# Spectral filter and squared-ReLU feed-forward, two layers on one core: paired evictions of the inverse transform, split banks for the first two tiles, outer and inner quarters for the last tile of layer 1

## The chip, the core and the metric

The kernel runs on one core of a Trainium2 chip. The core's engines work through their own lists of instructions and wait for each other by semaphores: TensorE (PE in the profile, its weight loads PEld), VectorE (DVE), ScalarE (ACT), GpSimd (POOL) and SyncE (SP, which here issues most of the DMAs). Matrix products go to PSUM, which has eight banks of 512 float32 per partition, and ACT or DVE copy them from there to SBUF ("evict" them). The metric is the device time of one execution in microseconds (us), as the median of several runs.

## The reference

`x` is 2048 x 448 in bf16. Four blocks follow one another; A is a spectral filter with a residual, B a feed-forward network with a residual, and each has its own normalisation in front:

```python
def _A_ref(x, w_r, w_i):
    X = rfft2(x.astype(float32), axes=(-2, -1))
    X = X * (w_r + 1j * w_i)
    return irfft2(X, s=(S, D), axes=(-2, -1)).astype(bfloat16)

def _B_ref(x, w1, b1, w2, b2):
    h = einsum("bsd,df->bsf", x, w1) + b1
    r = where(h > 0, h, 0)
    return einsum("bsf,fd->bsd", r * r, w2) + b2

x = x + _A_ref(_layernorm(x), A_w_r, A_w_i)
x = x + _B_ref(_layernorm(x), B_w1, B_b1, B_w2, B_b2)
x = x + _A_ref(_layernorm(x), A_w_r, A_w_i)
x = x + _B_ref(_layernorm(x), B_w1, B_b1, B_w2, B_b2)
```

S is 2048, D is 448, the filter's weights are 2048 x 225, and the hidden width is 1792.

## The kernel before

**Tiling.** The sequence index is split as 128 partitions times 16 tiles, `s = 16 p + t`, so a tile `t` holds every sixteenth row. A transform of length 2048 is then one of length 128 over partitions and one of length 16 over tiles. Along D the code first forms sums and differences of `x[d]` and `x[447-d]`, and for layer 2 of their halves again, so that the products over D have 224 or 112 columns (`HD` = 224, `QD` = 112).

**Stages of a spectral block.** `A1` (layer 1) and `A2` (layer 2) normalise a tile and make the first transform: a tile's statistics (`ln_stats`, `act_stats`, `ln_rstd`) give a scaled copy `Fs` of the constant matrix `FA_sb`, on POOL, ACT or DVE; the products go to a bank and are evicted to `XA`. `TD` is the transform over D of one pair of the eight pairs of sequence frequencies, evicted to the arena. `B` is the part over 16, evicted to the arena as well. `W` multiplies by the complex weights `Wt`, all on DVE. `Bi` is the inverse over 128: for a pair p two banks (`lb` 0 and 1) of four matmuls each, evicted to `VT`. `TI` is the inverse over D by tiles, evicted to `TIo` (in the profile `tmp`), and `AI` the last inverse step, added to `x` by DVE into `x_sb` (L1104). The pairs run in the order 1 to 7, 0; `Bi0.n` is the n-th in layer 1, `Bi1.n` in layer 2, so n = 7 is pair 0. A pair's Bi needs W's products for that pair.

**Stages of a feed-forward block.** `ln_B` squares and sums a tile (`Square` with an accumulator, L1128, on ACT) and sets up the normalisation; the tile is transposed into `yT` (by matmuls for tiles 0 and 1, later by DMA). `h` makes the hidden columns: matmuls with `W1_sb`, relu on ACT, square on DVE. The first hidden matmuls (`h0.0`, `h1.0`) need tiles 0 and 1 alone. `o` multiplies by `W2_sb` and adds the residual (L1245, `o_tile`). In layer 1 each `o` tile is followed by its `A2` work for layer 2: `ln_stats`, sums and differences into `xin`, a second level of them into `yA`, and `second_A`'s four matmuls of 128 columns into a bank, evicted to `XA` by ACT. The last tile, t = 15, has its 448 output columns cut into two halves (`CUT`), so that the first half's work overlaps the second half's matmuls. `TD1.0` is the first that needs `XA` of all 16 tiles.

**What sets the order.** The program is written as a list of small units of work, numbered as they are created, each with its engine, its reads and writes, and a cost. A planner can order them by those costs, but here `ORDER` holds a finished order: for each engine the unit numbers in the sequence in which they are issued, PE, ACT, DVE, POOL and SP each on its own. `EV` and `op.alt` say which engines may take a unit; the list in which its number stands decides. Costs and priorities (`PR`) therefore do not change what is issued. Banks are handed out along that order. `warm_mm` (L1352) adds matmuls on ones that only keep PE busy: 16 at the start, 9 more in waits.

**Start.** POOL clears `ones`, then the last block of `W1_sb`, makes the indices `ix`, gathers two blocks of the filter's weights by indirect DMA, makes four reversed copies of x (`XR`), clears the padding of `x_sb`, and then scales the first `Fs`. The clearing of the padding of `Z` in the arena (128 x 1024) is its last instruction. SP issues the loads one after another and holds the two loads of `Wt` that wait for the gathers, and what stands behind them. `b1in` (the bias of the hidden layer) is loaded early; its transposing matmul stands between layer 1's TD and B products, before TD0.5.

Of the kernel before, what the change touches and what calls it, by code (L numbers as in the profile page):

```python
# [6 lines left out]
ALU = mybir.AluOpType  # L7
# [17 lines left out]
VB_PAIRS = (2, 3, 4, 5)  # L25

# [98 lines left out]
1384 1389 1394 1399 1410 1404 1407 1413 1416""",  # L125
    "act": """
# [12 lines left out]
1306 1308 1303 1170 1171 1174 1177 1178 1377 1372 1370 1380 1375 1387 1382 1385 1392 1390 1397 1395 1400 1402""",  # L139
    "dve": """  # L140
# [108 lines left out]
def _res(a):  # L249
    return a.ap() if isinstance(a, _PsAP) else a  # L250
# [1180 lines left out]
```

## Time and profile before

| | us |
|---|---|
| median of 3 runs | 269.94 |
| lowest, highest | 269.80, 269.97 |
| profiled execution | 269.8 |
| its span in the profile | 267.9 |
| granted clock of PE | 1.00 |

The page of the profile gives busy times over the whole span. PE is busy for nearly all of it, so what matters more is the busy time by stage: a stage whose PE column nearly equals its length is bound by PE, and in the others another engine's column, or a chain between the engines, sets the length. The seams are: 0 to 18.6 us the loads, statistics and A1; to 43.5 TD, B, W and Bi of layer 1; to 56.4 TI and AI with the first hidden matmuls; to 137.1 the feed-forward network; to 146.3 the last tile and the rest of A2; to 161.5 TD, B and W of layer 2; to 168.9 Bi1; to 175.5 TI and AI up to the first hidden matmul; to 265.5 the second network; and then the last store.

In a timeline row the columns are the start, the time until the last of the grouped instructions ends, the engine, the line, the operation, the tiles, the shapes and the count. In square brackets stands how long the engine had been idle before, and which engine and line ended that.

### The profile page before, as it was taken

The numbers are of one execution on the slowest core, as the hardware profiler recorded it, in microseconds if no ns is written. First come the engines' busy times: TensorE is split into PE (matmuls) and PEld (weight loads), VectorE is DVE, ScalarE is ACT, GpSimd is POOL, SyncE is SP. The second block draws the span as 40 slices with busy tenths as digits, with TensorE's granted clock in tenths as the row PEclk, the third lists the DMA queues.
The fourth block names the chain that finished last, engine by engine and source line by source line (L and its number), as shares of the span: only waits on it lengthen the run. The fifth ranks groups of instructions, "written<-read, shape, count | busy, mean of one in ns | idle before, by whom it ended". The sixth has DMA issues, their size and how long they took to land.

```text
span 267.9 us, 5691 instructions
## 1 busy us (share of the span) xinstructions
PE 256.9 (96%) x2090; PEld 165.1 (62%) x2090; DVE 203.7 (76%) x724; ACT 175.6 (66%) x393; POOL 14.9 (6%) x31
## 2 busy tenths in 40 slices
PE   8789998999999999999998998899999999999996
PEld 3667587778544555655567766688654675554454
DVE  3978996999999976299997899689995059734442
ACT  5977899987279746784226897899445885040930
POOL 8940000000000000000000000000000000000000
PEclk9999999999999999999999999999999999999999
DMA  7999410022300215000000000001423100023103
GB/s 232 404 291 347 157 40 1 3 40 42 66 10 20 41 22 107 4 0 2 1 0 2 2 0 0 4 14 30 78 60 68 42 0 0 20 39 92 52 0 103
DMA packets 25554, 16.33 MB, mean 61 GB/s; under 512 B 18186, under 2 KB 24566, under 8 KB 25528
## 3 DMA queue, kind: packets, MB, share of 16 engines
q1 hardware_dynamic: 24792, 14.26, 19.7%
q10 hardware_dynamic: 576, 0.92, 0.9%
q0 software_dynamic: 160, 0.81, 0.7%
q8 instruction: 16, 0.26, 0.4%
q14 instruction: 10, 0.08, 0.1%
HBM read 10.46 MB, written 1.84 MB: 46 GB/s over the span
## 4 chain that ended last, share of the span: by engine, by line
PE 76%; DVE 11%; ACT 7%; POOL 2%; issue 2%; DVEq 0%; ACTq 0%; POOLq 0%
PE ps L675 76%; ACT VT L700 4%; DVE tmp L729 4%; DVE arena L729 2%; DVE x_sb L1104 1%; ACT arena L700 1%; POOL Wt L772 1%; DVE x_sb L1245 1%; ACT arena L694 1%; DVE VT L729 1%; ACT XA L700 1%; DVE st L834 1%; POOL VT L701 1%; POOL W_sb L742 1%; ACT VT L1128 0%
## 5 line engine op out<-in xcount | busy, mean ns | idle before, releaser
L675 PE MATMUL ps<-yT,W_sb 64*128 64x512 bf16 (+1 forms) x770 | 90.2, 346 | 0.1
L675 PE MATMUL ps<-W_sb,arena 128*128 128x448 bf16 (+3 forms) x476 | 87.1, 342 | 0.0
L675 PEld LDWEIGHTS ps<-yT,W_sb 64*128 64x128 bf16 (+1 forms) x770 | 56.2, 95 | 30.3 <-ACT arena L694 1.6
L675 PEld LDWEIGHTS ps<-W_sb,arena 128*128 128x128 bf16 x476 | 45.5, 98 | 38.5 <-DVE arena L729 1.6
L729 DVE TENSOR_TENSOR arena<-arena 128x512 bf16<-128x512 bf16 (+1 forms) x140 | 45.2, 365 | 25.3 <-ACT arena L694 24.9
L694 ACT ACTIVATE arena<-ps,b1col 128x512 bf16<-128x512 f32 x84 | 51.7, 692 | 18.1 <-PE ps L675 17.9
L1128 ACT ACTIVATE VT<-x_sb 128x448 bf16<-128x448 bf16 x32 | 18.5, 581 | 22.4 <-DVE x_sb L1104 22.4
L700 ACT ACTIVATE arena<-ps 128x448 bf16<-128x448 f32 (+1 forms) x42 | 26.2, 723 | 6.0 <-PE ps L675 5.9
L1245 DVE SCALAR_TENSOR_TENSOR x_sb<-ps,arena 128x448 bf16<-128x448 f32 (+3 forms) x26 | 14.7, 582 | 12.5 <-PE ps L675 12.2
L694 ACT ACTIVATE mv<-mv,epst 128x1 f32<-128x1 f32 (+1 forms) x41 | 11.7, 296 | 16.9 <-DVE mv L835 10.8
L700 ACT ACTIVATE XA<-ps 128x512 bf16<-128x512 f32 x28 | 15.3, 594 | 6.0 <-PE ps L675 5.9
L694 ACT ACTIVATE arena<-ps 128x256 bf16<-128x256 f32 x56 | 17.8, 400 | 1.3 <-PE ps L675 1.3
L675 PE MATMUL ps<-arena,G_sb 128*128 128x448 bf16 (+1 forms) x84 | 17.0, 335 | 0.4 <-ACT arena L700 0.4
L675 PE MATMUL ps<-H_sb,arena 128*128 128x256 bf16 x128 | 16.2, 273 | 1.2 <-DVE arena L729 0.8
L675 PE MATMUL ps<-yT,VT 64*128 64x512 bf16 x42 | 15.8, 376 | 0.0
L700 ACT ACTIVATE VT<-ps 128x512 bf16<-128x512 f32 (+1 forms) x30 | 14.5, 631 | 1.4 <-PE ps L675 1.4
L729 DVE TENSOR_TENSOR tmp<-arena,Wt 128x896 bf16<-128x896 bf16 x26 | 14.8, 622 | 0.4 <-ACT arena L700 0.4
L675 PEld LDWEIGHTS ps<-H_sb,arena 128*128 128x128 bf16 x128 | 11.9, 98 | 5.1 <-DVE arena L729 3.3
L700 ACT ACTIVATE tmp<-ps 128x896 bf16<-128x896 f32 (+1 forms) x18 | 14.1, 850 | 1.4 <-PE ps L675 1.4
L675 PE MATMUL ps<-TD_sb,XA 112*128 112x112 bf16 (+1 forms) x184 | 13.9, 229 | 1.0 <-ACT XA L700 1.0
L675 PEld LDWEIGHTS ps<-TD_sb,XA 112*128 112x128 bf16 (+1 forms) x184 | 12.3, 98 | 2.8 <-DVE XA L701 1.2
L1104 DVE SCALAR_TENSOR_TENSOR x_sb<-ps,x_sb 128x448 bf16<-128x448 f32 x16 | 9.8, 620 | 4.5 <-PE ps L675 4.5
(89 smaller groups left out, 295.4 us busy)
## 6 DMA issues: line engine op xcount, KB each, us to landing
out_dram<-x_sb SPq DMA_DIRECT2D x15, 112.0 KB, 1.8
W_sb<-in_B_w_dram SPq DMA_DIRECT2D x1, 1568.0 KB, 10.1
W_sb<-in_B_w_dram SPq DMA_DIRECT2D x1, 1344.0 KB, 10.3
xin<-in_A_x_dram ACTq DMA_DIRECT2D x4, 224.0 KB, 4.8
xin<-in_A_x_dram SPq DMA_DIRECT2D x4, 224.0 KB, 4.2
H_sb<-c_H SPq DMA_DIRECT2D x1, 896.0 KB, 9.4
G_sb<-c_G SPq DMA_DIRECT2D x1, 672.0 KB, 7.9
Wt<-in_A_w_i_dram SPq DMA_DIRECT2D x1, 393.8 KB, 7.3
```

The costliest lines, as they stand in the source:

```text
L675: return sch.add("pe", lambda e: e.matmul(_res(o), lhsT, rhs, start=start, stop=stop, skip_group_check=skip), [lhsT, rhs], [o], cost=cost, ...
L694: sch.add("act", lambda e: e.activation(o, _res(i), func, **kw), rd, [o], cost=c)
L700: op = sch.add(engs[0], lambda e: e.activation(o, _res(i), ACT.Copy) if h[0].eng == "act" else e.tensor_copy(o, _res(i)), [i], [o], cost=c ...
L701: e.tensor_copy(o, _res(i)), [i], [o], cost=c[engs[0]], unit=unit)
L729: sch.add(eng, lambda e: e.tensor_tensor(o, _res(a), b, op), [a, b], [o], cost=_free(o) / rate + 69.0)
L742: sch.add(eng, lambda e: e.memset(o, v), [], [o], cost=_free(o) / 1.92 + 60.0)
L772: sch.add("pool", lambda e: e.indirect_dma_start(o, None, (A_w_r, A_w_i)[i], bass.IndirectOffsetOnAxis(ix[:], 0)), [ix[:]], [o], is_dma=Tr ...
L834: small(lambda e, si=si, xi=xi: e.bn_stats(si, xi), [xi], [si], _free(xi) / 0.96 + 69.0)
L1104: small(lambda e, xx=xx, xi=xi, r=r, i=i: e.scalar_tensor_tensor(out=xx, in0=_res(r), scalar=1.0, in1=xi, op0=ALU.mult, op1=ALU.add, accum ...
L1128: sch.add("act", lambda e, i=i, o=o, x=x: e.activation(o, x, ACT.Square, accum_out=sd[:, i, 1:2]), [x], [o, sd[:, i, 1:2]], cost=560.0)
L1245: small(lambda e: e.scalar_tensor_tensor(out=o, in0=_res(i), scalar=r[0] if r else 1.0, in1=xb[:, t, d0:d1], op0=ALU.mult, op1=ALU.add), [ ...
```

## The change

1. `MERGE`: for the Bi pairs 1 to 5 the two banks are taken as one tile of two adjacent banks, with one eviction of 128 x 1024 in place of two of 128 x 512.
2. `stage_TI` for single tiles (tiles 0 and 1): its two halves g = 0 and 1 go to two banks with two matmuls each, each evicted by itself (128 x 224) by ACT or DVE.
3. Tile 15 of layer 1: `CUT` now holds the outer quarters (columns 0 to 111 and 336 to 447, as one strided part) and the inner half (112 to 335). The sums and differences of mirrored columns (`fold`) follow each part at once; the statistics use the same parts.
4. `second_A` of tile 15 uses two banks and eight matmuls of 64 columns; each half (eight of the 16 frequencies) is evicted by itself by ACT or DVE.
5. The Square of tiles 0 and 1 may run on DVE (`scalar_tensor_tensor` with an accumulator). In the new order it does so for both tiles in layer 1 and for tile 0 in layer 2.
6. Some cost constants of the planner are others, which the fixed order does not use.
7. `ORDER` is new for all engines. At the start the clearing of Z stands second on POOL, ahead of W1's clearing and the gathers; the two gathers are swapped, with the clearing of `x_sb` between them; both loads of `Wt` behind the gathers now wait for the later gather or come after a load that does; XR.14 moves from ACT to POOL; `b1in`'s load moves behind the `W1u` loads of layer 1 on SP, and its matmul to just before `h0.1`. There are 26 warm matmuls instead of 25.

The count of PE's instructions goes from 2090 to 2095, ACT's units from 358 to 347, DVE's from 692 to 699, POOL's from 27 to 28.

```diff
+MERGE = (1, 2, 3, 4, 5)
...
     "pool": """
-12 17 14 15 16 20 13 19 22 21 52 60 76 25 105 68 92 84 141 144 23 115 118 24 157 154 18""",
+12 18 17 14 16 13 15 19 20 22 21 68 52 60 76 102 25 92 84 141 144 26 23 118 24 131 157 154""",
...
         def stage_Bi(p, first):
-            q = [_Tile(1), _Tile(1)]
             if p > 0:
                 z = Z[:, 4 * p:4 * p + 4, :]
+                m = _Tile(2) if p in MERGE else None
                 for lb in range(2):
+                    q = m or _Tile(1)
+                    k = lb if m else 0
...
-                    evac(VT[:, lb, :, :, 2 * p:2 * p + 2, :],
-                         q[lb][lambda b: ps[:, b, :].rearrange("p (g t c j) -> p g t c j", g=2, t=16, c=2)], EV["Bi"])
+                    if not m:
+                        evac(VT[:, lb, :, :, 2 * p:2 * p + 2, :],
+                             q[lambda b: ps[:, b, :].rearrange("p (g t c j) -> p g t c j", g=2, t=16, c=2)], EV["Bi"])
+                if m:
+                    evac(VT[:, :, :, :, 2 * p:2 * p + 2, :].rearrange("p a g t c j -> p (a g t) (c j)"),
+                         m[lambda b: ps[:, b:b + 2, :].rearrange("p a (t c) -> p (a t) c", c=16)], EV["Bi"])
...
         def stage_TI(t, n, late):
+            if n == 1:
+                for g in range(2):
+                    q = _Tile(1)
+                    for r in range(2):
+                        mm(q[lambda b: ps[:, b, 0:HD]], VT[0:QD, r, g, t].rearrange("p c j -> p (c j)"), TI_sb[:, r, g, :],
+                           r == 0, r == 1)
+                    evac(TIo[:, t, g, :], q[lambda b: ps[:, b, 0:HD]], EV["TI1"])
+                return
...
+                if t < NFLIP:
+                    op.alt = {"act": 575.0, "dve": 545.0}
...
-        def o_tile(t, d0, d1):
+        def o_tile(t, cut):
...
         def second_A(t):
-            q = _Tile(1)
+            n = 2 if t == NT - 1 else 1
+            q = [_Tile(1) for _ in range(n)]
+            w = P // n
...
+            for i in range(n):
+                c = slice(16 // n * i, 16 // n * (i + 1))
+                evac(XA[:, :, :, c, 8 * t:8 * t + 8].rearrange("p k g c j -> p (k g) c j"),
+                     q[i][lambda b: ps[:, b, 0:4 * w].rearrange("p (k c j) -> p k c j", k=4, j=8)], EV["A2" if n == 1 else "A1"])
...
-        CUT = ((0, HD), (HD, D)) if HALVES else ((0, D),)
+        CUT = (lambda a: a.rearrange("p (k d) -> p k d", k=4)[:, 0:4:3], lambda a: a[:, QD:3 * QD])
...
+        def fold(t, d0, d1):
+            w = xin[:, t, :].rearrange("p (g d) -> p g d", g=2)
+            a, b = x_sb[:, t, d0:d1], x_sb[:, t, D - 1 - d0:D - 1 - d1:-1]
+            tt(w[:, 0, d0:d1], a, b, ALU.add)
+            tt(w[:, 1, d0:d1], a, b, ALU.subtract)
...
+                        elif t == NT - 1:
+                            fold(t, QD * k, QD * (k + 1))
```

More of the change, by code (lines that the diff above doesn't have):

```diff
@@ L175 @@
 LOOK = {}
-EV = {'A1': ['act', 'dve'], 'A2': ['act'], 'TD': ['act', 'dve'], 'B': ['act', 'dve'], 'Bi': ['act', 'dve'], 'Bi0': ['act', 'dve'], 'TI': ['act'], 'M': ['act', 'dve'], 'T': ['act', 'dve'], 'XR': ['pool', 'act', 'dve'], 'FS': ['pool', 'act', 'dve'], 'FS2': ['dve'], 'XN': ['act', 'dve']}
+EV = {'A1': ['act', 'dve'], 'A2': ['act'], 'TD': ['act', 'dve'], 'B': ['act', 'dve'], 'Bi': ['act', 'dve'], 'Bi0': ['act', 'dve'], 'TI': ['act'], 'TI1': ['act', 'dve'], 'M': ['act', 'dve'], 'T': ['act', 'dve'], 'XR': ['pool', 'act', 'dve'], 'FS': ['pool', 'act', 'dve'], 'FS2': ['dve'], 'XN': ['act', 'dve']}
 SPLIT = (1, 2, 4)
@@ L830, in ln_stats @@
                 x = xin[:, t, :] if mean else x_sb[:, t, 0:D]
-                n = len(CUT) if t == NT - 1 and not mean else 1
+                cuts = CUT if t == NT - 1 and not mean else WHOLE
+                n = len(cuts)
                 for i in range(n):
-                    xi, si = (x[:, CUT[i][0]:CUT[i][1]] if n > 1 else x), st[:, t, 6 * i:6 * i + 6]
+                    xi, si = cuts[i](x), st[:, t, 6 * i:6 * i + 6]
                     small(lambda e, si=si, xi=xi: e.bn_stats(si, xi), [xi], [si], _free(xi) / 0.96 + 69.0)
@@ L1127, in ln_B @@
                 x = x_sb[:, i, 0:D].rearrange("p (a c) -> p a c", a=4)
-                sch.add("act", lambda e, i=i, o=o, x=x: e.activation(o, x, ACT.Square, accum_out=sd[:, i, 1:2]),
-                        [x], [o, sd[:, i, 1:2]], cost=560.0)
+                h = []
+                op = sch.add("act", lambda e, i=i, o=o, x=x, h=h: e.activation(o, x, ACT.Square, accum_out=sd[:, i, 1:2])
+                             if h[0].eng == "act" else e.scalar_tensor_tensor(
+                                 out=o, in0=x, scalar=1.0, in1=x, op0=ALU.mult, op1=ALU.mult, accum_out=sd[:, i, 1:2]),
+                             [x], [o, sd[:, i, 1:2]], cost=575.0)
+                h.append(op)
+                if t < NFLIP:
+                    op.alt = {"act": 575.0, "dve": 545.0}
             if t >= 4:
@@ L1235, in h_part, with r @@
                 tt(hb, hb, hb, ALU.mult)
[L1237 removed]
+        def o_tile(t, cut):
             hb = hbuf[(t // 4) % 2]
             q = _Tile(1)
+            o, xi = cut(x_sb[:, t, 0:D]), cut(xb[:, t])
+            n = _free(o)
+            def r(a):
+                return a if len(list(o.ap)) == 2 else a.rearrange("p (k d) -> p k d", k=2)
             for fb in range(FB):
[L1241 removed]
+                mm(q[lambda b: r(ps[:, b, 0:n])], hb[:, fb, (t % 4) * P:(t % 4 + 1) * P], cut(W2_sb[:, fb, :]),
                    fb == 0, fb == FB - 1)
[L1243 to L1247 removed]
+            i = q[lambda b: r(ps[:, b, 0:n])]
+            rs = [r2[:, t, 0:1]] if t < 4 else []
+            small(lambda e: e.scalar_tensor_tensor(out=o, in0=_res(i), scalar=rs[0] if rs else 1.0, in1=xi,
+                                                   op0=ALU.mult, op1=ALU.add), [i, xi] + rs, [o], n / 0.96 + 69.0)
         def second_A(t):
@@ L1256, in second_A @@
                     d = (2 * k + g) * QD
-                    mm(q[lambda b, d=k * 2 * P + g * P: ps[:, b, d:d + P]], yA[:, t % 8, d:d + P], f,
-                       k == 0 and g == 0, k == 1 and g == 1, skip=True)
-            A_out(t, q, EV["A2"])
-        CUT = ((0, HD), (HD, D)) if HALVES else ((0, D),)
-        CUT2 = ((0, 3 * QD), (3 * QD, D)) if HALVES else ((0, D),)
+                    for i in range(n):
+                        mm(q[i][lambda b, d=(2 * k + g) * w: ps[:, b, d:d + w]], yA[:, t % 8, d:d + P], f[:, w * i:w * (i + 1)],
+                           k == 0 and g == 0, k == 1 and g == 1, skip=True, unit=u)
+            for i in range(n):
+                c = slice(16 // n * i, 16 // n * (i + 1))
+                evac(XA[:, :, :, c, 8 * t:8 * t + 8].rearrange("p k g c j -> p (k g) c j"),
+                     q[i][lambda b: ps[:, b, 0:4 * w].rearrange("p (k c j) -> p k c j", k=4, j=8)], EV["A2" if n == 1 else "A1"])
+        WHOLE = (lambda a: a,)
+        CUT = (lambda a: a.rearrange("p (k d) -> p k d", k=4)[:, 0:4:3], lambda a: a[:, QD:3 * QD])
+        CUT2 = (lambda a: a[:, 0:3 * QD], lambda a: a[:, 3 * QD:D])
         TGROUPS = [(0, 1), (1, 1), (2, 2), (4, 2), (6, 2), (8, 2), (10, 2), (12, 2), (14, 2)]
@@ L1313, in ffn @@
                     sch.bias, sch.tag = 5500.0 * (NT - t), f"o{L}.{t}"
-                    for d0, d1 in ((CUT2 if last else CUT) if t == NT - 1 else ((0, D),)):
-                        o_tile(t, d0, d1)
+                    for k, cut in enumerate((CUT2 if last else CUT) if t == NT - 1 else WHOLE):
+                        o_tile(t, cut)
                         if last:
-                            dma("sp", out_dram[:, t, d0:d1], x_sb[:, t, d0:d1])
+                            dma("sp", cut(out_dram[:, t, :]), cut(x_sb[:, t, 0:D]))
+                        elif t == NT - 1:
+                            fold(t, QD * k, QD * (k + 1))
                     if not last:
@@ L1321, in ffn @@
                         w = xin[:, t, :].rearrange("p (g d) -> p g d", g=2)
[L1322 removed]
                         y = yA[:, t % 8, 0:D].rearrange("p (k g d) -> p k g d", k=2, g=2)
                         ln_stats([t])
[L1325 to L1326 removed]
+                        if t < NT - 1:
+                            fold(t, 0, HD)
                         for k in range(2):
```

31 lines of the change are left out of this document (12 added, 19 removed), and 94 rows, old and new, of the table ORDER.

## The prediction

> **What bounds the kernel now.** I read the page first, then the busy time by stage, then the timeline at the seams between the stages.
>
> ```profile
> span 267.9 us, 5691 instructions
> ```
> ```profile
> PE 256.9 (96%) x2090; PEld 165.1 (62%) x2090; DVE 203.7 (76%) x724; ACT 175.6 (66%) x393; POOL 14.9 (6%) x31
> ```
> ```profile
> PE 76%; DVE 11%; ACT 7%; POOL 2%; issue 2%; DVEq 0%; ACTq 0%; POOLq 0%
> ```
>
> The chain that ended last lies on PE for 76%, and on DVE, ACT and POOL for 20%. Those 20% are what a new order of the same work can touch. By stage (columns: length, then busy time and instructions of each engine):
>
> ```profile
> 18.60:43.50 24.90, 24.12 (x198) 17.52 (x198) 22.89 (x44) 21.05 (x39) 0.00 (x0) 1.00 0.51 160
> 43.50:56.40 12.90, 12.20 (x137) 10.58 (x138) 10.54 (x46) 12.38 (x31) 0.00 (x0) 1.00 0.01 2
> 56.40:137.10 80.70, 80.66 (x611) 46.85 (x612) 69.17 (x288) 50.14 (x117) 0.00 (x0) 1.00 0.14 30
> 137.10:146.30 9.20, 8.49 (x80) 6.13 (x78) 7.88 (x39) 4.29 (x10) 0.00 (x0) 1.00 0.01 2
> 146.30:161.50 15.20, 14.20 (x171) 10.56 (x171) 13.50 (x26) 13.46 (x23) 0.00 (x0) 1.00 0.00 1
> 161.50:168.90 7.40, 6.28 (x51) 4.67 (x51) 6.86 (x14) 5.98 (x13) 0.00 (x0) 1.00 0.00 1
> 168.90:175.50 6.60, 5.88 (x76) 5.06 (x76) 4.42 (x20) 5.86 (x13) 0.00 (x0) 1.00 0.01 4
> 175.50:265.50 90.00, 90.00 (x676) 54.14 (x676) 55.45 (x193) 47.84 (x111) 0.00 (x0) 1.00 0.18 43
> ```
>
> Both feed-forward stages (56.40 to 137.10 and 175.50 to 265.50) are PE without a gap, and the change leaves their matmuls as they are. They are 170.7 us in which nothing can be won. In the other rows PE's idle time is 0.78, 0.70, 0.71, 1.00, 1.12 and 0.72 us, together 5.0; the start before 18.60 comes on top. So the whole matter is a few tenths at each seam.
>
> **The change part by part.** A time named "before" is that of the profiled execution (269.8 us: the span of 267.9 and 1.9 around it). The order of all five engines is new, so I follow each seam through the new order with the durations of before.
>
> *Start.* The clearing of Z (the arena's 128x1024) moves on POOL from behind all Fs to the second place, ahead of W1's clearing, both gathers, the XR copies and the first Fs.
>
> ```profile
> 16.56 0.95 POOL L742 MEMSET arena<- 128x1024 bf16 x1
> ```
> ```profile
> 1.00 5.84 PE L1352 MATMUL ps<-ones 128*128 128x512 bf16 x16 [1.00 <-POOL ones L742]
> 8.27 0.27 PE L675 MATMUL ps<-Fs,xin 128*128 128x256 bf16 x1 [1.43 <-POOL Fs L712]
> ```
> ```profile
> 13.61 0.27 PE L675 MATMUL ps<-Fs,m 128*128 128x256 bf16 x1
> ```
> ```profile
> 17.35 0.27 PE L675 MATMUL ps<-Fs,m 128*128 128x256 bf16 x1
> ```
> ```profile
> 18.62 1.31 PE L675 MATMUL ps<-TD_sb,XA 128*128 128x224 bf16 x12 [1.00 <-ACT XA L700]
> ```
>
> PE's first useful matmul waits for POOL's Fs, and POOL works through its list without a pause up to there, so the 0.95 us stand on the path: first matmul at 9.2 instead of 8.27. From 8.27 to 13.61 are 49 steps of 0.109 us. At that pace the 80 matmuls of A1 would have had their last start at 8.27 + 79 x 0.109 = 16.88, but it was at 17.35: 0.47 us of stalls, because the later tiles' statistics were late. Those are computed from loads that do not move, so a start 0.95 later absorbs the stalls: 0.95 - 0.47 = +0.48. The move of XR.14 from ACT to POOL frees ACT near the end, so I take +0.42. Bounds: +0.1 (the last evictions, not PE, set the 18.62) and +0.95 (all stalls stay). DVE is busy 22.89 of the next 24.90, PE 24.12, and both do the same work after, so the shift is carried to the inverse transform.
>
> The second gather now comes about 1 us later, and SP holds both Wt loads, and all loads queued behind them (W1, TI, W2), until it has landed.
>
> ```profile
> 11.38 0.38 SPq L667 DMA_DIRECT2D Wt<-in_A_w_r_dram  x1
> ```
> ```profile
> Wt<-in_A_w_r_dram SPq DMA_DIRECT2D x1, 393.8 KB, 7.8
> ```
> ```profile
> 22.52 0.63 DVE L729 TENSOR_TENSOR tmp<-tmp,Wt 128x896 bf16<-128x896 bf16 x1
> ```
>
> Issued at 12.4 the later one lands at 12.4 + 7.8 = 20.2, 2.3 us ahead of its first use at 22.52. Cost 0; with this cover gone, a microsecond for a microsecond.
>
> *Merged evictions (five pairs).* A step from one 128x512 eviction to the next, and one from 128x896 to the next, come from these two rows:
>
> ```profile
> 144.09 2.06 ACT L700 ACTIVATE XA<-ps 128x512 bf16<-128x512 f32 x4
> ```
> ```profile
> 156.95 3.50 ACT L700 ACTIVATE arena<-ps 128x896 bf16<-128x896 f32 x4
> 163.28 5.56 ACT L700 ACTIVATE VT<-ps 128x512 bf16<-128x512 f32 x12 [1.36 <-PE ps L675]
> ```
>
> With a last duration of 0.62 the first gives (2.06 - 0.62) / 3 = 0.48; with 1.10 the second gives (3.50 - 1.10) / 3 = 0.80. The 384 columns between them cost 0.32, so 1024 columns take 0.80 + 128 x 0.32 / 384 = 0.91 against 2 x 0.48 = 0.96: 0.05 us a pair, 0.25 a layer. In layer 1 the end of the inverse hangs on pair 7, whose weights DVE finishes last, so the 0.25 are slack; Bi0.5 now stands ahead of Bi0.7 on PE, +0.08 (bounds -0.1 and +0.25). In layer 2 ACT is back to back from 163.28, but pair 7 binds there too, see below.
>
> [...]
>
> *Split first inverse tiles (TI), Squares on DVE.* In layer 1:
>
> ```profile
> 43.04 0.26 PE L675 MATMUL ps<-TI_sb,VT 112*128 112x224 bf16 x1 [0.49 <-DVE VT L701]
> 43.53 1.62 PE L675 MATMUL ps<-TI_sb,VT 112*128 112x224 bf16 x23 [0.24 <-ACT VT L700]
> 44.99 0.55 PE L675 MATMUL ps<-tmp,FI_sb 128*128 128x224 bf16 x4
> ```
> ```profile
> 45.58 0.62 DVE L1104 SCALAR_TENSOR_TENSOR x_sb<-ps,xin 128x448 bf16<-128x448 f32 x1 [2.12 <-PE ps L675]
> ```
> ```profile
> 47.27 0.61 ACT L1128 ACTIVATE VT<-x_sb 128x448 bf16<-128x448 bf16 x1
> ```
> ```profile
> 47.83 0.60 ACT L1128 ACTIVATE VT<-x_sb 128x448 bf16<-128x448 bf16 x1
> ```
>
> From 43.50 to 56.40 ACT is busy 12.38 of 12.90, the most of any stage. Two Squares leave it, each 47.83 - 47.27 = 0.56 of its time: ACT 11.3. On DVE I price them alike (its 128x448 read of PSUM at 45.58 takes 0.62): 10.54 + 1.1 = 11.6. Before, the first AI0 stood behind TI0.1, TI0.0, TI0.10 and TI0.14 on PE and started at 44.99. After, only TI0.1, half of TI0.0 and TI0.10 stand ahead, and its two halves are evicted side by side by ACT and DVE: I get 44.4 for it, and 45.8 instead of 46.15 for the second. The way to the first hidden matmul shortens by 0.4 to 0.5; TI0.12 falls behind it. I take -0.4; bounds -0.6 and 0.
>
> *Tile 15's quarters and A2 in two halves.*
>
> ```profile
> 145.09 0.40 PE L675 MATMUL ps<-Fs,tmp 128*128 128x128 bf16 x4 [0.19 <-DVE tmp L738]
> ```
> ```profile
> 146.24 1.44 PE L675 MATMUL ps<-TD_sb,XA 112*128 112x112 bf16 x26
> ```
>
> DVE closes the layer without a pause, and the quarters have the same elements in smaller pieces; which piece is late changes, the end, which lets PE go at 145.09, does not: 0. Then came four matmuls and one 512-column eviction (0.62 alone) to 146.24. Now eight matmuls of 64 columns (+0.1) and 256 columns, 0.62 - 256 x 0.32 / 384 = 0.41 alone, of which the first TD units need only ACT's: -0.15. Bounds +0.1 and -0.4 (DVE's half stands behind TD1.0's eviction, used only from TD1.4 on, 3 us later).
>
> *Weights of layer 2.* DVE is the bound there.
>
> ```profile
> 154.23 1.16 DVE L729 TENSOR_TENSOR tmp<-tmp 128x896 bf16<-128x896 bf16 x2
> 155.49 1.16 DVE L729 TENSOR_TENSOR arena<-tmp 128x896 bf16<-128x896 bf16 x2
> 156.57 2.23 DVE L729 TENSOR_TENSOR tmp<-arena,Wt 128x896 bf16<-128x896 bf16 x4
> ```
> ```profile
> 159.79 0.62 DVE L729 TENSOR_TENSOR tmp<-arena,Wt 128x896 bf16<-128x896 bf16 x1
> ```
>
> Two instructions take 1.08 when the next follows at once (155.49 to 156.57), but 154.23 to 155.49 is 1.26: the second sum's reader waits for it. The new order puts a W1.4 product in between: -0.18. B1.5 and B1.6, which the product at 159.79 needs, are evicted in the new order by 159.4, so I get no new wait. Bounds -0.4 and +0.3 (TD1.3's late evictions hold B1.3 on PE by 0.5, and ACT then falls behind). Bi1 follows DVE to pair 7, so it moves along with it.
>
> *TI of layer 2.* Before it started at 168.49 behind the last VT eviction; the same split and reordering bring the first hidden matmul forward by about 0.1, since DVE now has a Square (0.56) between its reads of AI1.1 and AI1.2: -0.1, bounds -0.3 and +0.3.
>
> Sum: +0.42 + 0.08 - 0.40 + 0 - 0.15 - 0.18 - 0.10 = -0.33. On the profiled 269.8 that is 269.5; the median of the runs lies 0.14 above that execution, so 269.6 for a median.
>
> **The rivals.**
> 1. *The clearing is hidden.* If XA's evictions and not PE set 18.62 (PE waited 1.00 there for ACT), the start costs about 0 and the rest stays: -0.75, 269.2. For it: that wait; against: the evictions follow their matmuls, so they move along.
> 2. *DVE becomes the late engine at the two TI seams (the slower side).* Each Square that now stands between two reads of PSUM holds PE's next TI unit, whose banks those reads free. From the point at which DVE's 2.12 us of idle before 45.58 no longer covers the added 1.1 us, the two gains (-0.5) turn into losses of one Square each (0.56): -0.33 + 0.5 + 1.1 = +1.27, 271.2; if only one layer tips, -0.33 + 0.25 + 0.56 = +0.48, 270.4. Against it: 11.6 of 12.9 leaves 1.3 us.
> 3. *b1in's wait.* Its load moves from the start to behind layer 1's weight transfers on SP, and its matmul to just before h0.1 on PE, where every matmul is queued behind it.
>
> ```profile
> 70.74 1.38 SPq L667 DMA_DIRECT2D VT<-in_B_w_dram  x2
> ```
> ```profile
> VT<-in_B_w_dram SPq DMA_DIRECT2D x1, 192.0 KB, 3.3
> ```
> ```profile
> 75.45 0.55 PE L675 MATMUL ps<-tmp,FI_sb 128*128 128x224 bf16 x4
> ```
>
> Issued at 70.74 + 1.38 = 72.1 it lands by 75.4 even if it takes the 3.3 us of the large one; the new order needs it at about 75.5. From 1 us more it makes the kernel slower: 270.6.
> 4. *PE's clock falls in the longer wait before 9.2.* PE idles 1.43 us ahead of 8.27 and keeps its pace; it would idle 2.4. At 0.109 for 256 columns the 16 first matmuls of 512 would take 3.5, but took 5.84: they lost 2.35 to a lower clock at their start. The same again: 269.6 + 2.35 = 272.0. [...]
>
> **How the numbers follow.** About 0.2% (0.54 us) is what a measurement can tell from no change, so "same" is 269.40 to 270.48. Forecast 0.48 (its own range 269.1 to 270.1), rival 1 0.27, rival 2 0.15, rival 3 0.05, rival 4 0.05. Faster: a third of the forecast's share and nine tenths of rival 1's, 0.40. Slower: rival 4 (0.05), most of 3 (0.03), two thirds of 2 (0.10): 0.18. Same: 0.42. Range 268.7 to 270.7: the terms' bounds, which are independent, with rival 1 and half of rival 2.
>
> **What would show it.** The first A1 matmul at 9.2 and TD0's first at 19.0; ACT's 128x1024 rows at some 0.91 a step; the stage from TI0's first matmul to the first hidden one 0.4 shorter; TD1.0 some 0.15 sooner after the last DVE work; no 0.18 hole at W1.4; the feed-forward stages 80.7 and 90.0 as before. A PE wait for b1in, or a wait of PE for DVE at TI1.8, would make it wrong; so would a start that costs nothing.

## The result, and the profile after

| | before | after |
|---|---|---|
| median, us | 269.94 | 271.44 |
| lowest, highest (16 executions each) | 269.80, 270.17 | 270.14, 271.72 |
| ratio of the times, 95% interval | | 1.0038 [1.0024, 1.0051] |
| profiled execution, us | 269.8 | 271.68 |
| its span, us | 267.9 | 269.7 |
| its granted clock of PE | 1.000 | 0.994 |

The changed kernel is slower by 0.38% in the mean of its executions (the medians lie 1.50 us apart), more than the 0.2% that the prediction took as the limit of what can be told, and outside its range. Its 16 executions fall in two groups, and the granted clock parts them: seven at 270.14 to 270.16 with a clock of 1.000, nine at 271.42 to 271.72 with 0.994. So there are two things to explain: 0.2 us that every execution pays, and 1.5 us that nine of them pay on top. The profiled one is of the nine.

The page of after: the span, the busy times, and PE's granted clock in 40 slices, tenths of full speed.

```profile
span 269.7 us, 5702 instructions
...
PE 258.3 (96%) x2095; PEld 168.6 (63%) x2095; DVE 205.1 (76%) x734; ACT 174.2 (65%) x379; POOL 15.4 (6%) x32
...
PEclk9799999999999999999999999999999999999999
```

The second slice is the only one below full. Busy time by stage, cut at the seams of before moved to where they lie now (columns: stretch, length, then busy time of PE, PEld, DVE, ACT, POOL, then PE's clock, the DMA share and GB/s), A1 of before ahead of it:

```profile
8.27:18.60 10.33, 9.22 (x80) 7.44 (x81) 9.01 (x38) 9.55 (x25) 7.79 (x16) 1.00 1.08 359
```
```profile
9.08:20.80 11.72, 10.72 (x80) 8.43 (x80) 8.08 (x35) 8.46 (x22) 7.40 (x16) 0.85 1.05 338
20.80:45.65 24.85, 23.98 (x199) 17.63 (x200) 22.74 (x44) 20.92 (x33) 0.00 (x0) 1.00 0.43 135
45.65:58.25 12.60, 12.01 (x139) 10.76 (x138) 11.48 (x51) 12.02 (x31) 0.00 (x0) 1.00 0.01 2
58.25:139.55 81.30, 80.46 (x611) 48.30 (x609) 69.42 (x289) 47.75 (x112) 0.00 (x0) 1.00 0.15 29
139.55:148.50 8.95, 8.25 (x83) 6.11 (x81) 7.86 (x42) 4.90 (x12) 0.00 (x0) 1.00 0.01 2
148.50:163.70 15.20, 15.13 (x181) 11.43 (x180) 13.80 (x27) 13.29 (x21) 0.00 (x0) 1.00 0.00 1
163.70:171.10 7.40, 6.07 (x48) 4.03 (x46) 6.79 (x14) 6.34 (x10) 0.00 (x0) 1.00 0.00 1
171.10:177.40 6.30, 5.80 (x76) 5.08 (x77) 5.06 (x23) 5.55 (x12) 0.00 (x0) 1.00 0.01 3
177.40:267.30 89.90, 89.89 (x677) 54.71 (x676) 55.08 (x193) 49.01 (x112) 0.00 (x0) 1.00 0.18 43
```

Two rows have grown: A1 (from 10.33 to 11.72, with a clock of 0.85) and the first feed-forward network, which took 80.70 with PE busy for 80.66 and now takes 81.30 with 80.46. All later rows are as long as before or shorter.

The start in the timeline of after, first POOL and then PE:

```profile
0.86 0.95 POOL L743 MEMSET arena<- 128x1024 bf16 x1
8.46 1.84 POOL L713 TENSOR_SCALAR Fs<-FA_sb,rstd 128x256 bf16<-128x256 bf16 x4
```
```profile
0.98 6.04 PE L1393 MATMUL ps<-ones 128*128 128x512 bf16 x16 [0.98 <-POOL ones L743]
9.08 0.27 PE L676 MATMUL ps<-Fs,xin 128*128 128x256 bf16 x1 [2.07 <-POOL Fs L713]
...
9.30 0.27 PE L676 MATMUL ps<-Fs,xin 128*128 128x256 bf16 x1
9.41 0.30 PE L676 MATMUL ps<-Fs,VT 128*128 128x256 bf16 x1
9.52 0.41 PE L676 MATMUL ps<-Fs,m 128*128 128x256 bf16 x1
...
12.71 0.39 PE L676 MATMUL ps<-Fs,m 128*128 128x256 bf16 x1
12.92 0.28 PE L676 MATMUL ps<-Fs,xin 128*128 128x256 bf16 x1
13.04 0.27 PE L676 MATMUL ps<-Fs,VT 128*128 128x256 bf16 x1
```

The early clearing has pushed POOL's first Fs back, and with it PE's first A1 matmul from 8.27 to 9.08; PE's idle time ahead of that has grown from 1.43 to 2.07 us (2.23 in the expectations below, which count from where one more matmul on ones could have started). The matmuls begin at full pace (0.11 a step) and from 9.52 to 12.92 they take twice as long: 16 steps in 3.40 us where 16 x 0.109 = 1.74 would do. Of the 1.66 lost, 1.5 remain at the end of A1 (20.83 against 19.30 for TD0.0 in a kernel below that starts A1 at the same time); a stall in A1 takes up the rest.

The feed-forward network of layer 1 in after, ACT and PE:

```profile
64.88 0.59 ACT L1146 ACTIVATE VT<-x_sb 128x448 bf16<-128x448 bf16 x1
...
65.44 0.59 ACT L1146 ACTIVATE VT<-x_sb 128x448 bf16<-128x448 bf16 x1
...
66.00 0.67 ACT L695 ACTIVATE arena<-ps 128x256 bf16<-128x256 f32 x2
```
```profile
63.28 2.46 PE L676 MATMUL ps<-yT,W_sb 128*128 128x256 bf16 x21
66.45 0.56 PE L676 MATMUL ps<-tmp,FI_sb 128*128 128x224 bf16 x4 [0.71 <-ACT arena L695]
```

PE waits 0.71 us at AI0.8 for a bank that a relu of h0.0.2 frees. In the new order that relu stands on ACT behind the Squares of tiles 6 and 7. (An expectation below has 0.87 at 65.47: that is the time from the last matmul's start less its step of 0.11.) The wait is a new one, in a stage that the prediction took over unchanged.

First starts at the seams, from the timelines; the last three columns are kernels of the experiments, all at full clock.

| us | before | after | after, 24 matmuls on ones | after, late clearing | and earlier relu |
|---|---|---|---|---|---|
| A1 | 8.27 | 9.08 | 9.08 | 8.22 | 8.22 |
| TD0.0 | 18.62 | 20.83 | 19.30 | 18.43 | 18.44 |
| TI, layer 1 | 43.04 | 45.17 | 43.63 | 42.76 | 42.77 |
| h0.0.0 | 50.56 | 51.87 | 50.34 | 49.46 | 49.47 |
| h0.1 | 75.93 | 78.60 | 77.08 | 76.19 | 75.54 |
| TD1.0 | 146.24 | 148.47 | 146.94 | 146.05 | 145.56 |
| TI, layer 2 | 168.49 | 170.68 | 169.15 | 168.25 | 167.68 |
| h1.0.0 | 175.49 | 177.37 | 175.85 | 174.94 | 174.38 |
| last matmul | 265.30 | 267.08 | 265.57 | 264.65 | 264.10 |

### The profile page after: what moved, and what is told of

Its sections match the earlier page's. It is cut to its first block, busy times and chain, and to the rows that moved or that the text cites. A ratio compares the mean times of both kernels' runs of the same rounds, so it can differ in the third digit from the quotient of the medians.

```text
span 269.7 us, 5702 instructions
## 1 busy us (share of the span) xinstructions
PE 258.3 (96%) x2095; PEld 168.6 (63%) x2095; DVE 205.1 (76%) x734; ACT 174.2 (65%) x379; POOL 15.4 (6%) x32
## 5 line engine op out<-in xcount | busy, mean ns | idle before, releaser
L676 PEld LDWEIGHTS ps<-yT,W_sb 64*128 64x128 bf16 (+1 forms) x770 | 58.1, 95 | 27.9 <-ACT arena L695 1.2
L1146 ACT ACTIVATE VT<-x_sb 128x448 bf16<-128x448 bf16 x29 | 16.6, 577 | 8.2 <-DVE x_sb L1121 8.2
L701 ACT ACTIVATE XA<-ps 128x512 bf16<-128x512 f32 (+1 forms) x28 | 15.3, 589 | 9.1 <-PE ps L676 9.1
L676 PE MATMUL ps<-arena,G_sb 128*128 128x448 bf16 (+1 forms) x84 | 17.6, 335 | 0.3 <-ACT arena L701 0.3
L676 PE MATMUL ps<-H_sb,arena 128*128 128x256 bf16 x128 | 15.1, 273 | 0.7 <-DVE arena L730 0.6
L701 ACT ACTIVATE VT<-ps 128x1024 bf16<-128x1024 f32 (+2 forms) x20 | 14.0, 785 | 0.9 <-PE ps L676 0.9
L676 PE MATMUL ps<-TI_sb,VT 112*128 112x112 bf16 (+1 forms) x128 | 10.2, 224 | 2.0 <-ACT VT L701 0.9
```

Source lines behind the costliest of these rows:

```text
L676: return sch.add("pe", lambda e: e.matmul(_res(o), lhsT, rhs, start=start, stop=stop, skip_group_check=skip), [lhsT, rhs], [o], cost=cost, ...
L701: op = sch.add(engs[0], lambda e: e.activation(o, _res(i), ACT.Copy) if h[0].eng == "act" else e.tensor_copy(o, _res(i)), [i], [o], cost=c ...
L1146: op = sch.add("act", lambda e, i=i, o=o, x=x, h=h: e.activation(o, x, ACT.Square, accum_out=sd[:, i, 1:2]) if h[0].eng == "act" else e.sc ...
```

## The experiments

Each kernel ran several times beside the kernel before on the same chip; a ratio is against that kernel there, with its 95% interval. Three chips were used, on which the kernel before has medians of 269.98, 269.90 and 269.95, so a difference of under 0.1 us between times from two chips says nothing. Where an edit of `ORDER` is shown, it is a part of a line.

### The clearing of Z last on POOL again

```diff
-12 18 17 14 16 13 15 19 20 22 21 68 52 60 76 102 25 92 84 141 144 26 23 118 24 131 157 154""",
+12 17 14 16 13 15 19 20 22 21 68 52 60 76 102 25 92 84 141 144 26 23 118 24 131 157 154 18""",
```

> The kernel after, with one thing undone: the clearing of Z stands last on POOL again, as in the kernel before; every other order is that of after. Theory T (the early clearing delays the first A1 matmul, and the idle time of 2.23 us that it makes ahead of it is what lets PE's clock fall): first A1 matmul at about 8.3 us instead of 9.08, idle time ahead of it about 1.4, granted clock 1.00 in every run, a median of about 269.4, which is 270.15 (the runs of after at full clock) less 0.7. Rival R (the clock falls because of something else in the new order, which only shows in the first 13 us): the runs still part into two groups 1.5 us apart, near 269.4 and 270.9, with clocks of 1.00 and 0.994.

Measured: 269.29 (269.09 to 269.32, six executions, all at a clock of 1.000), ratio 0.9971 [0.9959, 0.9983]. First A1 matmul at 8.22 behind 1.43 us of idle time. Theory T holds, R falls: one instruction's place costs 0.86 us (270.15 against 269.29) and the clock. Without it the rest of the change makes the kernel faster.

### The early clearing alone, in the kernel before

```diff
-12 17 14 15 16 20 13 19 22 21 52 60 76 25 105 68 92 84 141 144 23 115 118 24 157 154 18""",
+12 18 17 14 15 16 20 13 19 22 21 52 60 76 25 105 68 92 84 141 144 23 115 118 24 157 154""",
```

> The kernel before, with one thing of the change alone: the clearing of Z stands second on POOL. Theory T: first A1 matmul at about 9.1 us instead of 8.27, 2.2 us of idle ahead of it; the runs part into two groups, at full clock some 0.5 to 0.8 above the kernel before (270.4 to 270.7) and at 0.994 another 1.5 above that (about 272.0). Rival R: one group at 270.4 to 270.7 with a clock of 1.00 in every run. Rival of the prediction (the clearing is hidden): about 269.9 in every run.

Measured: four executions at 270.75 to 270.92 (clock 1.000) and two at 271.85 and 272.00 (0.994), median 270.89, ratio 1.0045 [1.0029, 1.0061]. Both costs come from this one move; the price at full clock, 0.9, was above what was expected. The clearing isn't hidden.

### More and fewer matmuls on ones ahead of A1

The first edit adds eight matmuls on ones behind the 16 at the start of after (`self.extra` is 8), and a second kernel has it with two in place of eight. The second edit makes a third kernel, which ends the start after 12.

```diff
+                if self.extra and u.tiles:
+                    for _ in range(self.extra):
+                        bk = pick_banks(1, start)
+                        d = _Op("pe", self.warm_fn(bk[1], 512), False, 216.0, 195.0)
+                        self.ops["pe"].append(d)
+                    self.extra = 0
```
```diff
+                    if cold and len(self.ops["pe"]) >= 12:
+                        break
                     if gap < 120.0 or not (cold or recent < self.warm_share * self.WINDOW):
                         break
```

24 matmuls:

> The kernel after, with eight more matmuls on ones ahead of the first A1 matmul, 0.22 us each, so that PE's idle time there shrinks from 2.23 to about 0.5 us; the clearing of Z stays early. Theory T (idle time is the cause): first A1 matmul at about 9.1 as in after, clock 1.00 in every run, 270.15 in every run. Rival L (not the idle time but the later start, or the work on the other engines, lets the clock fall): two groups as in after, near 270.15 and 271.65.

18 matmuls:

> The kernel after with 18 matmuls on ones at the start instead of 16: 0.43 us less idle time, so about 1.65 instead of 2.07 in a run in which the clock rises as late as in the profile of after. Theory S: in the worst stretch PE is busy for (3.41 - 1.65) / 3.41 = 52%, so no run falls, 270.15 in every run. Rival I (any idle time above the 1.43 us of the kernel before is at risk): some runs at 271.65, fewer than 9 of 16.

12 matmuls:

> The kernel after with 12 matmuls on ones at the start instead of 16; the clearing of Z stays early, so PE is idle for some 3 us ahead of the first A1 matmul. Theory S (PE's clock is set anew every 3.4 us by the share of that stretch in which PE worked: in after 1.35 of 3.41 us, 40%, let it fall, and in the kernel before with the early clearing 54% twice kept it): nearly every run falls, 271.6 to 272 at a clock of 0.994 or less, and few or none at 270.15. Rival W (a stretch must be wholly without work for the clock to fall): the idle time is rarely a whole 3.4 us at the right moment, so most runs stay at 270.15, fewer low ones than in after (9 of 16).

| matmuls on ones at the start | executions | of them at a lower clock | times, us |
|---|---|---|---|
| 24 | 11 | 0 | 270.15 to 270.20 |
| 18 | 11 | 0 | 270.12 to 270.18 |
| 16 (after) | 16 | 9 | 270.14 to 270.16, 271.42 to 271.72 |
| 12 | 5 | 5 | 271.46 to 271.70 at 0.994, 272.40 at 0.987 |

A1 starts at 9.08 in all four, and the other engines do the same work: so L falls. W (a stretch wholly without work) falls with five low executions of five, and I (any idle time above 1.43 us) with none of eleven. In these four kernels it is PE's own work ahead of A1 that decides. The matmuls on ones are 0.427 apart at first and then 0.216, and the one in between gives the moment of the change. In after the matmuls on ones reach full pace at 6.12, and half pace runs from 9.53 to 12.94: 3.41 us at full pace, then 3.41 at half. With 12 matmuls full pace comes at 3.70, half pace is there when A1 starts and ends at 13.94, three times 3.41 later. Cut at these points, after and the kernel with 12 read (length, PE's busy time first, and its granted clock behind POOL's column):

```profile
6.12:9.53 3.41, 1.34 (x10) 0.70 (x9) 3.41 (x19) 3.16 (x13) 3.40 (x8) 1.00 1.07 397
9.53:12.94 3.41, 3.41 (x19) 2.35 (x17) 1.52 (x10) 1.73 (x6) 2.52 (x6) 0.50 1.03 411
12.94:16.35 3.41, 3.41 (x33) 3.06 (x32) 2.69 (x12) 2.67 (x7) 2.58 (x7) 1.00 1.00 343
```
```profile
3.70:7.11 3.41, 1.37 (x7) 0.39 (x4) 2.54 (x9) 2.54 (x9) 3.13 (x5) 1.00 1.04 372
7.11:10.52 3.41, 1.44 (x7) 1.02 (x8) 2.95 (x17) 2.30 (x11) 3.19 (x7) 0.50 1.07 399
10.52:13.93 3.41, 3.41 (x17) 2.35 (x16) 1.59 (x9) 2.16 (x7) 1.88 (x4) 0.50 1.03 421
```

The stretches in which PE worked for 1.34, 1.37 and 1.44 us (39 to 42%) are followed by one at 0.50, the two at 0.50 in which it worked for all of 3.41 by full pace. Stretches of the same length from the rise to full pace, for the kernel before with the early clearing (full pace there from 4.14), the kernel with 18 matmuls (from 6.36), the kernel before (from 5.84), and the kernel of the next experiment (from 6.95) read:

```profile
4.14:7.55 3.41, 1.90 (x10) 0.69 (x7) 2.85 (x14) 2.81 (x9) 3.10 (x6) 1.00 1.05 356
7.55:10.96 3.41, 1.80 (x17) 1.65 (x18) 2.74 (x12) 2.31 (x9) 3.23 (x7) 1.00 1.07 410
10.96:14.37 3.41, 3.41 (x33) 2.99 (x32) 2.71 (x14) 3.41 (x12) 3.09 (x8) 1.00 1.01 412
```
```profile
6.36:9.77 3.41, 1.90 (x13) 1.04 (x12) 3.14 (x17) 2.68 (x11) 3.40 (x8) 1.00 1.05 393
```
```profile
5.84:9.25 3.41, 1.98 (x16) 1.20 (x14) 3.39 (x20) 3.08 (x13) 3.41 (x9) 1.00 1.05 391
```
```profile
6.95:10.36 3.41, 1.69 (x15) 1.21 (x14) 3.23 (x20) 3.19 (x13) 3.41 (x8) 1.00 1.07 396
```

With 1.69 to 1.98 us of work (50 to 58%) in these stretches, none of these profiled executions shows a clock below 1.00. The three rows of the first of these kernels are the strongest: PE is idle there for 3.12 us in one piece ahead of A1, longer than the 2.07 in after, and its clock stays at 1.00; the cut at 7.55 falls into the middle of the idle time and leaves 1.90 and 1.80 us of work to either side. The rise from which these stretches are counted lies between 3.70 and 6.95 in the profiled executions, with 12 to 18 matmuls on ones from the same moment on. That it also differs between executions of one program, so that some of them fall and others don't, is the author's estimate: of each program one execution was profiled, and a low and a full one of the same program were not set side by side. The 69 executions of the kernel before, those of the result among them, show no low one (270.40 at most). Between 42 and 50% no stretch was seen.

### One step of ACT's statistics ahead of an Fs

The kernel before with the early clearing, and on ACT the scaled Fs of A1.6 (102) behind the statistics of A1.5 and A1.4 (88, 81, 89):

```diff
-5 7 2 9 11 71 55 56 49 57 72 99 73 87 65 102 88 81 89 26 138 ...
+5 7 2 9 11 71 55 56 49 57 72 99 73 87 65 88 81 89 102 26 138 ...
```

> The kernel before with the early clearing of Z (270.75 to 270.92 at full clock), and one more edit: on ACT the scaled Fs for A1.6, which waits for PE to free its buffer, stands behind the statistics of A1.4 and A1.5 and not ahead of them. Theory Q (the 0.47 us of stalls were not absorbed because those statistics queue on ACT behind that Fs, and so move along with PE's start): DVE's wait of 1.25 us for ACT at 11.56 shrinks to under 0.5, the stalls in A1 shrink, and TD0's first matmul comes at 19.0 to 19.3 instead of 19.52; the runs at full clock lie 0.2 to 0.5 lower. Rival (the stalls come from the Fs buffers or from POOL's own list, which move along with PE anyway): TD0's first stays at 19.5.

Measured: five executions at full clock at 270.15 to 270.36, against 270.75 to 270.92; four at 0.994, 271.60 to 272.03. TD0's first matmul at 19.04. ACT's Fs and the first reciprocals behind it on DVE, in the kernel before, with the early clearing, and with this edit:

```profile
9.09 0.51 ACT L711 ACTIVATE Fs<-FA_sb,rstd 128x256 bf16<-128x256 bf16 x1 [0.30 <-PE ps L675]
...
10.66 0.22 DVE L865 RECIPROCAL rstd<-mv 128x1 f32<-128x1 f32 x2 [0.44 <-ACT mv L694]
```
```profile
9.98 0.51 ACT L711 ACTIVATE Fs<-FA_sb,rstd 128x256 bf16<-128x256 bf16 x1 [1.10 <-PE ps L675]
...
11.56 0.23 DVE L865 RECIPROCAL rstd<-mv 128x1 f32<-128x1 f32 x2 [1.25 <-ACT mv L694]
```
```profile
9.97 0.51 ACT L711 ACTIVATE Fs<-FA_sb,rstd 128x256 bf16<-128x256 bf16 x1 [0.22 <-PE ps L675]
...
10.33 0.19 DVE L865 RECIPROCAL rstd<-mv 128x1 f32<-128x1 f32 x2
```

Theory Q holds. The Fs waits for PE to free its buffer, the statistics wait behind it in ACT's list, and DVE waits for those: a later PE makes them later in turn. With the statistics ahead, this wait of DVE is gone, A1 has no stall left (8.62 us from its first to its last matmul, 79 steps of 0.109), and TD0 comes 0.48 sooner. Whether the edit alone would also speed up the kernel before wasn't tried: its reciprocals come at 10.66, later than the 10.33 here, so a part of the 0.48 may be a gain of this order and not an absorbed delay.

In after that Fs has another place. There, with 24 matmuls on ones, the first instruction on ACT that waits for PE ahead of statistics is an eviction of A1:

```profile
9.82 0.60 ACT L708 ACTIVATE XA<-ps 128x512 bf16<-128x512 f32 x1 [0.56 <-PE ps L683]
```

With the late clearing it starts at 9.47. The first reciprocal behind it on DVE moves from 10.34 to 10.64, the later ones from 13.93 to 14.80 and from 14.99 to 15.86, by the whole 0.87, and A1 takes 8.95 us from its first to its last matmul against 8.94 with the late clearing: no stall is absorbed. No order of ACT was tried in after itself.

### The relu ahead of the Squares

On top of the late clearing, 505 (the relu of h0.0.2) stands ahead of 361 and 360 (the Squares of tiles 6 and 7) on ACT:

```diff
-... 538 361 360 505 520 ...
+... 538 505 361 360 520 ...
```

> The first kernel of this set with one more edit: on ACT the relu of h0.0.2 stands ahead of the two Squares of tiles 6 and 7 (L1146), not behind them. Theory S (the idle time of PE ahead of AI0.8, 0.87 us at 65.47 in after, comes from that relu waiting behind those Squares, and is where the gain at TI0 is given back): PE's idle time between o0.0 and h0.1 falls by 0.5 to 0.9 us and the median by as much, to 268.5 to 268.9. Rival C (ACT is the bound through that stretch, so the wait only moves to the next reader): the same idle time stands a few microseconds later and the median stays within 0.15 of the first kernel's.

Measured: 268.68 (268.40 to 268.70), ratio 0.9947 [0.9934, 0.9959]; the best of all kernels here, and faster than both. The stretch from TI's first matmul to h0.1 in the kernel before, with the late clearing, and with this edit too (length, PE's busy time):

```profile
43.04:75.93 32.89, 31.98 (x277) 23.91 (x278) 30.06 (x128) 23.95 (x69) 0.00 (x0) 1.00 0.15 32
```
```profile
42.76:76.19 33.43, 31.88 (x277) 23.96 (x279) 30.93 (x134) 22.37 (x64) 0.00 (x0) 1.00 0.15 32
```
```profile
42.77:75.54 32.77, 31.89 (x278) 23.98 (x279) 30.83 (x133) 22.11 (x63) 0.00 (x0) 1.00 0.16 33
```

PE's work is the same, about 31.9. The change had made the stretch 0.54 longer; the relu's new place brings 0.66 back, of which 0.55 reach the last matmul (264.10 against 264.65). S holds, C falls.

### The merged evictions undone

On top of the kernel with 268.68:

```diff
                 if m:
-                    evac(VT[:, :, :, :, 2 * p:2 * p + 2, :].rearrange("p a g t c j -> p (a g t) (c j)"),
-                         m[lambda b: ps[:, b:b + 2, :].rearrange("p a (t c) -> p (a t) c", c=16)], EV["Bi"])
+                    u = None
+                    for lb in range(2):
+                        u = evac(VT[:, lb, :, :, 2 * p:2 * p + 2, :],
+                                 m[lambda b, lb=lb: ps[:, b + lb, :].rearrange("p (g t c j) -> p g t c j", g=2, t=16, c=2)],
+                                 EV["Bi"], u)
...
```

> The kernel of the first set with the late clearing and the earlier relu (268.68), with the merged evictions of the inverse undone: the two adjacent banks are evicted one after the other, 128x512 each, in the same place of the same engine's list. Theory of the prediction (0.05 us a pair and slack, since pair 7 binds the end of the inverse): median within 0.1 of 268.68. [...]

Measured: 268.96 (268.93 to 268.98), 0.28 above, more than the 0.1 of the expectation, though on another chip; the last matmuls of the profiled executions lie 0.15 apart (264.25 against 264.10). ACT's rows with the merge, and without it:

```profile
35.37 2.86 ACT L701 ACTIVATE VT<-ps 128x1024 bf16<-128x1024 f32 x3
38.10 0.94 ACT L701 ACTIVATE arena<-ps 128x896 bf16<-128x896 f32 x1
```
```profile
35.35 3.04 ACT L701 ACTIVATE VT<-ps 128x512 bf16<-128x512 f32 x6
38.23 0.98 ACT L701 ACTIVATE arena<-ps 128x896 bf16<-128x896 f32 x1
```

Three pairs take 38.10 - 35.37 = 2.73 merged and 38.23 - 35.35 = 2.88 unmerged: 0.91 and 0.96 a pair, as predicted. That the saving is slack is not so in layer 1: TI starts at 42.77 with the merge and at 42.89 without. In layer 2 it is slack: the way from TD1.0 to TI takes 22.12 us with it and 22.11 without.

### The Squares of tiles 0 and 1 back on ACT in layer 1

On top of the kernel with 268.68 again, first ACT's list and then DVE's:

```diff
-... 275 298 277 397 279 315 304 331 306 285 ...
+... 275 298 277 397 279 315 301 304 331 282 306 285 ...
...
-... 296 300 302 301 303 281 311 307 283 282 284 ...
+... 296 300 302 303 281 311 307 283 284 ...
```

> The same kernel (268.68) with part 5 undone in layer 1: the Squares of tiles 0 and 1 stand on ACT again, behind TI0.2's and TI0.4's evictions. Theory P of the prediction (the Squares on DVE take 1.1 us off the engine that binds the stretch from TI to the first hidden matmul): that stretch grows by 0.2 to 0.5 and the median to 268.9 to 269.2. Rival N (PE has the same matmuls to do in that stretch and is idle for only 0.9 us of 32.8, so no engine's relief there is worth much): the first hidden matmul moves, the matmuls up to h0.1 end within 0.15 of the kernel with DVE's Squares, 268.5 to 268.85.

Measured: 269.46 (ten executions at 269.43 to 269.92 with a clock of 1.000, one at 271.13 with 0.994), 0.78 more, and 0.75 at the last matmul (264.85 against 264.10): further than P said, and N is wrong. The evictions of the transposed tiles on ACT, with the Squares on DVE, and on ACT:

```profile
47.37 0.49 ACT L701 ACTIVATE yT<-ps 128x384 bf16<-128x384 f32 x1
...
48.07 0.47 ACT L701 ACTIVATE yT<-ps 128x384 bf16<-128x384 f32 x1
```
```profile
46.38 0.57 ACT L1146 ACTIVATE VT<-x_sb 128x448 bf16<-128x448 bf16 x1
...
48.07 0.56 ACT L1146 ACTIVATE VT<-x_sb 128x448 bf16<-128x448 bf16 x1
...
48.62 0.48 ACT L701 ACTIVATE yT<-ps 128x384 bf16<-128x384 f32 x1
...
49.18 0.48 ACT L701 ACTIVATE yT<-ps 128x384 bf16<-128x384 f32 x1
```

The second of them is 1.11 later, and h0.0.0, which needs both tiles, starts at 50.60 instead of 49.47. All other orders are made for Squares on DVE here, so 0.78 is the price in this order, not that of part 5 in a kernel planned anew. The one low execution has the late clearing and 1.43 us of idle time like the kernel before; it wasn't profiled.

### Two more instructions of POOL behind the first Fs

On top of the kernel with 268.68, the clearing of x_sb (13) and XR.4 (21) leave the place ahead of the first Fs; 92 and 84 move ahead of 25, and the planner adds no matmul on ones inside A1.

```diff
-12 17 14 16 13 15 19 20 22 21 68 52 60 76 102 25 92 84 141 144 26 23 118 24 131 157 154 18""",
+12 17 14 16 15 19 20 22 68 52 60 76 13 102 92 21 84 25 141 144 26 23 118 24 131 157 154 18""",
...
+                    if 16 <= len(self.ops["pe"]) < 200:
+                        break
```

> The kernel with the late clearing and the earlier relu (268.68), and on POOL two more instructions moved from ahead of the first Fs to behind it: the clearing of x_sb's padding (0.33 us) and the copy XR.4 (0.5). Theory B (with the clearing of Z gone, POOL's list sets PE's start only by the last 0.2 us; DVE's first rstd, done at 7.36, is next): first A1 matmul at 7.95 to 8.1 instead of 8.22, median 268.4 to 268.7. Rival (POOL's list alone sets the start): first A1 matmul at 7.4, median at 267.9 to 268.1.

Measured: 268.86 (268.70 to 269.11), with the last matmul 0.25 later (264.35 against 264.10). The first A1 matmul came at 7.69, between the two theories, and neither time was met: TD0.0 starts at 18.71 instead of 18.44. A1 now begins 0.53 sooner and then waits for POOL, whose moved instructions stand between the Fs that A1 needs; the longest of its steps is 0.60 at 12.87. This set of moves gains nothing.

## Why the prediction was wrong

Two things failed: a fall of PE's clock that was held to be unlikely sets the median, and at full clock, too, the sign is wrong. There the change costs 0.2 us (270.15 against 269.94), where 0.33 was to be gained; that 270.15 lies inside the range doesn't make the sum right.

**The clock (rival 4).** It was on the list with a chance of 0.05, and it decided. It happens in 9 of 16 executions and sets the median. The step that failed is to take 2.4 us of idle time for nearly as harmless as 1.43, as that chance does: before showed a clock of 1.00 behind 1.43 us, and nothing showed it for 2.4. The number to compare was PE's work in the 3.41 us from the rise to full pace, 1.98 us (58%) and 1.34 (39%) in the profiled executions of before and after. The price of rival 4 was too high: it took what the matmuls on ones lose at the start (2.35), while here 3.41 us at half pace cost 1.5 us. That the start's loss is one of clock was the author's estimate from the pace (0.427 a matmul on ones, then 0.216): the column of the granted clock reads 1.00 from 0 to 8.27 in before.

**The start, +0.42.** At full clock it is +0.68 (19.30 against 18.62). The delay itself is 0.87 to 0.90 with nothing absorbed. The step that failed is "those are computed from loads that do not move": the statistics also queue on ACT behind instructions that wait for PE, an Fs in the order of before, an eviction in that of after. The edit that takes this Fs out of their way shows it for the order of before; for that of after it rests on the trace. That the start then costs the predicted 0.42 (19.04 against 18.62) is luck in part: the delay was 0.89 and not 0.95, and 0.06 of the prediction's sum were for XR.14, which that kernel doesn't move. The other edits of the start gained 0.19, as the late clearing shows (18.43 against 18.62); the prediction counted 0.06 there. First matmul at 9.2: it came at 9.08. Rival 1, the hidden clearing, falls; its 269.2 is what the kernel reaches without the clearing's move, 269.29.

**TI and the Squares of layer 1, -0.40.** The way to the first hidden matmul shrank by 0.82 (43.04 to 50.56 against 45.17 to 51.87), twice what was said. But it is mostly no gain: 85 matmuls stood ahead of h0.0.0, and 76 do now (TI0.12's eight and one on ones are behind it or gone). Over a stretch that has all of that work, TI to h0.1, after is 0.54 longer: the relu's new place takes 0.66 off, so without that wait a gain of 0.12 is left. Two steps failed: a milestone was read as time won though the matmuls behind it were other ones, and the feed-forward stage was taken over "as before", though ACT's order in it is new. Rival 2 had the sign, a loss at TI in one layer, but not the mechanism: PE waits for ACT's relu, not for DVE's read of PSUM. That the Squares belong on DVE here was right.

**The smaller terms.** Wt's gather at 0: TD0.0 to TI takes 24.34 in after and 24.42 before, so no wait. Bi0 at +0.08: it is -0.05, since Bi0's end lies 2.16 us later than before and TD0.0 2.22; 0.05 a pair was right to the digit (0.91 and 0.96), and calling it slack was wrong by about 0.1. Tile 15 and A2 at -0.15: o0.15's last matmul to TD1.0 takes 3.62 instead of 3.83, -0.21. W at -0.18: the hole at W1.4 is gone, but layer 2's Bi ends only 0.04 sooner after TD1.0. DVE's first products and its last sums in W take 1.27 and 1.25 until the next instruction in the kernel with the late clearing, against 1.20 and 1.19 before, which gives most of it back. TI of layer 2 at -0.10: -0.31 from its first matmul to h1.0.0 (6.69 instead of 7.00), a real gain, since 76 matmuls stand in both, and it lasts to the last matmul. Rival 3: b1in's load causes no wait of PE.

At full clock (the kernel with 24 matmuls on ones) the sum is +0.27 at the last matmul (265.57 against 265.30) instead of -0.33: the start is 0.26 worse than said, the stretch from the end of Bi0 to h0.1 0.92, W 0.14, and the rest 0.7 better, of which 0.23 lie between h0.1 and o0.15 (66.24 instead of 66.48 us for the same matmuls, with no visible wait in either). Where those 0.23 come from wasn't tried and stays open.

## What to carry to other kernels

Before an instruction is moved to the front of a list, follow what its delay makes late: the first user, the buffers that this user frees, and what stands in order behind whoever waits for them. A shorter way to a milestone is a gain only if the same work lies ahead of it; compare stretches with equal instructions, and check the new order inside the stages whose work stays the same. At a start with a wait ahead of PE, don't go by the length of the wait alone: here 2.07 us ended in half pace and 3.12 didn't, PE's work in stretches of 3.41 us parted the profiled executions (1.34 to 1.44 us against 1.69 and more), and two more matmuls of 0.22 us removed a loss of 1.5 us that hit 9 of 16 executions.

## What the runs showed of the hardware that was not expected

PE's granted clock stood at 0.50 for 3.41 us in the profiled execution of after (9.53 to 12.94) and for 6.82 in that of the kernel with 12 matmuls on ones (7.11 to 13.93). Ahead of these three stretches of 3.41 us at 0.50 PE had worked for 1.34, 1.37 and 1.44 us of the 3.41 before (39 to 42%); stretches with 1.69 to 1.98 us of work (50 to 58%) stood in profiled executions with a clock of 1.00 throughout. With 2.07 us of idle time ahead of A1 the clock fell to 0.50 in the execution of after, and with 3.12 us in one piece it stayed at 1.00 in that of the kernel before with the early clearing.
